# Attention stage of a three-block kernel: other slots for the head scaling, the weight chunks, the operand stacks and the big loads

## The chip, the cores and the metric

The kernel runs on one core of one Trainium2 chip. The metric is the device time of one execution in microseconds (us); lower is better. Engines are named as in the profile: PE (TensorE matmul), PEld (its weight load), DVE (VectorE), ACT (ScalarE), POOL (GpSimd), SP (SyncE, which here only issues DMAs).

## What is computed

Four sequences of 576 tokens go through attention with 8 heads of size 64, then a gated block that mixes over tokens, then a block with a low-rank token mixing and a wide feed-forward. The change touches the first block alone, and the conversion of the next block's weights that runs beside it.

```python
def _attn_ref(q, k, v):                      # (4, 8, 576, 64) each
    q_rot, k_rot = (rotate(q), rotate(k))    # rotary embedding
    scores = scale * np.matmul(q_rot, k_rot.transpose(0, 1, 3, 2))
    scores = scores - np.max(scores, axis=-1, keepdims=True)
    attn = np.exp(scores)
    attn = attn / (np.sum(attn, axis=-1, keepdims=True) + 1e-09)
    return np.matmul(attn, v)

def reference(...):
    x = attn_out.transpose(0, 2, 1, 3).reshape(B, S, H * D)
    x = _moe_ref(x=x, ...)     # h = gelu(x @ w_in); u * (w_sg @ norm(v) + b_sg); x + gated @ w_out
    return _moe2_ref(x=x, ...) # x + U V mixing over tokens, then x + relu(x @ w_ch1) @ w_ch2
```

## The kernel before

**Slots.** The attention stage has 32 heads, of 5 key chunks each (128 keys, the last 64). Its work is written out by hand in slots: head h takes slots 5h to 5h+4, and the loop over t runs from -20 to 162. In slot t PE does the scores of chunk t (`scores`, L245: the tile st), the row maxima of a tile 11 slots ahead (`row_max`, L216: the tile sm; DVE reduces it on L221) and the product with the values of the chunk three slots back (`values`, L273: pv). Row maxima of head h thus begin about slot 5h-11. Everything else is entered with `later(slot, fn)` and is issued at the end of its slot, in the order in which it was entered. A slot fixes only the order on each engine's queue; an engine runs its queue in order, and as early as its waits let it.

**PSUM.** The tiles st and sm share three buffers, so a scores matmul waits for the DVE maximum of the slot before it.

**One head's operands.** `load(h)` brings 576 KB into one of four buffers RAW. POOL rotates it in three steps (`rope`, L148 to L150). `stacks` then makes the stacked operands in three more steps: `high` rounds it on ACT (L162, tile K1) and has SP copy it twice (L163, L164); `low` subtracts on POOL (L167, tile K2), and SP copies K1 onto its own lower half (L168) and K2 into Q1 (L169); a last DMA writes a row of -1 (L173). The copy of K1 onto itself must wait until L163 and L164 have been read. Row maxima of the head need both copies of `low`. The six slots are 5h minus `LEAD`. `load(h)` is at slot 5h-30.

**A pair's scaling.** When the second head of pair i is through, at slot 10i+12 (t0), `finish` has SP gather the sums (`collect`, L304, two DMAs into rc); then POOL adds 1e-9 (`guard`, L307), DVE inverts (L310), SP writes the row to DRAM (L313) and reads it back spread over 64 partitions (L318, tile rb), and DVE scales the two heads (`apply`, L325, tile X). The slots after t0 are `INVERSE`; the second `apply` is one slot behind the first.

**Weights.** Eight chunks of w_in (512 KB each, doubles) and three smaller ones are loaded (L342) and converted: ACT (L71), DVE four times (L72 to L75), ACT (L350), POOL (L351). Chunk i loads in slot `MATRIX + APART * i` and its first step is `CONVERT` slots later. `raw64` has one buffer.

**SP is one queue.** All these DMAs but the row of maxima (L226, issued by ACT) stand in a single row on SP; if one waits for its data, all behind it wait.

After slot 162 the next block begins; from there on the order of all engines but PE is made by a scheduler.

Of the kernel before, what the change touches and what calls it, by code (L numbers as in the profile page):

```python
# [11 lines left out]
U32 = mybir.dt.uint32  # L12
# [17 lines left out]

LEAD = 23, 22, 19, 19, 15, 10
LEAD_IN = (-20, -19, -19, -8, -8, 1), (-19, -18, -16, -3, -1, 4), (-3, -3, 0, 2, 4, 8)
FIRST = (-17, -10), (-9, -9)

BY_ACT = (0, 1, 1, 1, 1), (1, 1, 0, 1, 1), (1, 0, 1, 1, 1)

LOAD, LOAD_FIRST, LOAD_V, SPLIT_V, SPLIT_V_FIRST = 30, -19, 16, (6, 1), (-11, -1)


AHEAD, RAMP_FROM, RAMP, MAX_1, ROW, ROW_0, ROW_1 = 11, -1, 25, -1, 2, -8, -9

INVERSE = 6, 8, 9, 12, 17

MATRIX, APART, CONVERT, ROWS = 12, 13, 5, (151, 159)


IDLE = 17, 2, 5, 0, 2, 5, 6, 1, 0, 1
# [3 lines left out]
def tile_kernel(ctx: ExitStack, tc: tile.TileContext, qk, vv, tabs, w_in, g_ln, wsgT, b_sg, w_out, u_r, v_r, w1, w2, out):  # L53
    nc = tc.nc

    def f(ap):
        return ap.bitcast(F32)
# [95 lines left out]
    def stacks(h, ticks):  # L153

        rot = RAW[h % NR][:, 0]
        K1, Q1, K2, Q2 = (t[h % NS] for t in (K1s, Q1s, K2s, Q2s))
        a, z = slice(0, D), slice(D, P)

        def high():
            nc.scalar.activation(K1, rot, AF.Copy)  # L162
            nc.sync.dma_start(f(Q1[a]), f(K1[z]))  # L163
            nc.sync.dma_start(f(Q2[a, 0:S]), f(K1[z]))  # L164

        def low():
            nc.gpsimd.tensor_tensor(K2, rot, f(K1), ALU.subtract)  # L167
            nc.sync.dma_start(f(K1[z]), f(K1[a]))  # L168
            nc.sync.dma_start(f(Q1[z]), f(K2[z]))  # L169
        if h < len(BY_ACT):  # L170
            steps = rope(nc.gpsimd, h) + first_stacks(h)
        else:
            steps = rope(nc.gpsimd, h) + (high, low, lambda: nc.sync.dma_start(f(K2[D:D + 1]), less_one))  # L173
            value_stacks(h)
        for tick, fn in zip(ticks, steps):
            later(tick, fn)
# [103 lines left out]
    def finish(h, t0):  # L280


        i = h // 2
        b, pr = divmod(i, NPAIR)
        o = (h % 2) * D
        pv = PVS.pop(h)[:, :, :HALF]
        if i < NP - 1:
            STAGE[h] = p1.tile([D + 1, S], F32, tag="stage", name=f"stage{h}", bufs=5)
            nc.scalar.activation(h2(STAGE[h]), pv[:D + 1], AF.Copy)
            sums = STAGE[h][D:D + 1]  # L290
        else:
            nc.scalar.activation(h2(X[b][o:o + D, pr]), pv[:D], AF.Copy)
            sums = STAGE[h] = p1.tile([1, S], F32, tag="stage", name=f"sums{h}", bufs=5)
            nc.vector.tensor_copy(h2(sums), pv[D:D + 1])  # L294
        if h % 2 == 0:
            return
        pool = p1 if i < NP - 1 else keep
        rc = pool.tile([P, 2 * S // P], F32, tag="rc", name=f"rc{i}", bufs=2 if i < NP - 1 else 1)
        rr = dram.tile([1, 2 * S], F32, tag="rr", name=f"rr{i}", bufs=2)

        def collect():
            for a in range(2):
                src = STAGE[h - 1 + a]
                nc.sync.dma_start(rc[a * D:(a + 1) * D], src[src.shape[0] - 1:])  # L304

        def guard():
            nc.gpsimd.tensor_scalar_add(rc, rc, 1e-9)  # L307

        def invert():
            nc.vector.reciprocal(rc, rc)  # L310

        def gather():
            nc.sync.dma_start(rr, rc)  # L313

        def spread():
            if i < NP - 1:
                RB[i] = p1.tile([D, 2, S], F32, tag="rb", name=f"rb{i}", bufs=1)
                nc.sync.dma_start(RB[i].rearrange("p a s -> p (a s)"), rr.to_broadcast([D, 2 * S]))  # L318
            else:
                for a in range(2):  # L320
                    nc.sync.dma_start(RB[i][a * D:(a + 1) * D], rr[:, a * S:(a + 1) * S].to_broadcast([D, S]))

        def apply(a):
            rows = slice(a * D, (a + 1) * D)
            nc.vector.tensor_tensor(X[b][rows, pr], STAGE.pop(h - 1 + a)[:D], RB[i][:, a], ALU.mult)  # L325

        def apply_last():
            nc.vector.tensor_tensor(X[b][:, pr], X[b][:, pr], RB[i], ALU.mult)
        later(t0, collect)
        for tick, fn in zip(INVERSE, (guard, invert, gather, spread)):  # L330
            later(t0 + tick, fn)
        if i < NP - 1:
            for a in range(2):
                later(t0 + INVERSE[4] + a, lambda a=a: apply(a))
        else:
            later(t0 + INVERSE[4], apply_last)

    def converted(t0, src, n, use):

        raw = p1.tile([P, 512, 2], U32, tag="raw64", name="raw64", bufs=1)[:, :n]  # L340
        t = p1.tile([P, 512], F32, tag="t64", name="t64", bufs=1)[:, :n]
        later(t0, lambda: nc.sync.dma_start(raw.rearrange("p n w -> p (n w)"), src))  # L342
        for j, fn in enumerate(from_f64(t, raw) + use(t)):
            later(t0 + CONVERT + j, fn)
# [28 lines left out]
    def later(t, fn):  # L373
        due.setdefault(t, []).append(fn)
# [31 lines left out]
    for h in range(2, NH):  # L406
        stacks(h, LEAD_IN[h - 2] if h < 5 else [NC * h - o for o in LEAD])
    for h in range(NR, NH):
        later(max(NC * h - LOAD, LOAD_FIRST + h), lambda h=h: load(h))
    WTICK = [MATRIX + APART * i for i in range(2 * KT + 3)]  # L410
    for i in range(2 * KT):
        w_in_chunk(WTICK[i], i)
# [504 lines left out]
```

## Time and profile before

| | |
|---|---|
| median of 3 runs | 968.64 us (966.61 to 969.42) |
| the profiled execution | 968.37 us, its span 966.6 us |
| PE busy | 929.6 us, 96% of the span |
| PEld / DVE / POOL / ACT busy | 81% / 54% / 40% / 36% of the span |
| attention stage | about 34 us (first scores) to 321 us (last pv) |

Busy shares are means over stages that differ. In the attention stage DVE and POOL are busy most of the time, and many short waits follow each other; so the stage is read by its period per head and by what ends PE's waits in it. A wait is put down to the engine whose signal came last; it is only as good as that guess, and SP's row of DMA issues has to be read beside it.

### The profile page before, as it was taken

The numbers are of one execution on the slowest core, as the hardware profiler recorded it, in microseconds if no ns is written. First come the engines' busy times: TensorE is split into PE (matmuls) and PEld (weight loads), VectorE is DVE, ScalarE is ACT, GpSimd is POOL, SyncE is SP. The second block draws the span as 40 slices with busy tenths as digits, with TensorE's granted clock in tenths as the row PEclk, the third lists the DMA queues.
The fourth block names the chain that finished last, engine by engine and source line by source line (L and its number), as shares of the span: only waits on it lengthen the run. The fifth ranks groups of instructions, "written<-read, shape, count | busy, mean of one in ns | idle before, by whom it ended". The sixth has DMA issues, their size and how long they took to land.

```text
span 966.6 us, 13198 instructions
## 1 busy us (share of the span) xinstructions
PE 929.6 (96%) x5180; PEld 784.4 (81%) x5180; DVE 524.3 (54%) x721; ACT 345.8 (36%) x550; POOL 382.6 (40%) x324
## 2 busy tenths in 40 slices
PE   6899998998999999999999899999999999999998
PEld 3687776777777898999999787888888888888887
DVE  7777787787875387333327945652652452222222
ACT  4366655665566453322315432321321230101000
POOL 7768776887852396232326542210210210000000
PEclk7899999999999999999999999999999999999999
DMA  5567868778751320000003001220220210000112
GB/s 174 149 180 167 203 167 187 185 176 196 170 138 38 109 79 1 1 1 1 23 23 109 22 22 44 90 85 1 82 93 1 66 44 0 1 1 22 44 49 82
DMA packets 58947, 78.00 MB, mean 81 GB/s; under 512 B 31403, under 2 KB 34758, under 8 KB 58886
## 3 DMA queue, kind: packets, MB, share of 16 engines
q1 hardware_dynamic: 58576, 77.08, 29.8%
q8 instruction: 41, 0.67, 0.3%
q14 instruction: 20, 0.16, 0.1%
q10 hardware_dynamic: 310, 0.08, 0.0%
HBM read 55.02 MB, written 4.79 MB: 62 GB/s over the span
## 4 chain that ended last, share of the span: by engine, by line
PE 73%; DVE 12%; DMA 8%; issue 3%; POOL 2%; ACT 1%; SPq 1%; ACTq 0%; DVEq 0%; POOLq 0%
PE a L544 20%; PE r L544 20%; PE pv L273 9%; PE st L245 6%; PE w L544 5%; DMA Q<-K 4%; PE m L544 3%; PE u L544 3%; PE v L544 3%; PE sm L216 3%; DVE MX L221 2%; DMA raw<-in_qk 2%; DVE X L325 1%; DVE t L74 1%; DVE g L625 1%
## 5 line engine op out<-in xcount | busy, mean ns | idle before, releaser
L221 DVE TENSOR_REDUCE MX<-sm 128x1 f32<-128x576 f32 (+1 forms) x160 | 118.6, 747 | 62.0 <-PE sm L216 59.4
L273 PE MATMUL pv<-pc,VV 128*65 128x288 f32 x512 | 144.8, 405 | 0.5 <-DVE sums L294 0.5
L245 PE MATMUL st<-Q,K 65*128 65x288 f32 (+3 forms) x640 | 126.8, 320 | 6.3 <-DVE MX L221 4.8
L245 PEld LDWEIGHTS st<-Q,K 65*128 65x128 f32 (+3 forms) x640 | 96.0, 179 | 20.0 <-DVE MX L221 7.5
L736 ACT ACTIVATE RH<-r 128x1024 fp32r<-128x1024 f32 (+1 forms) x38 | 35.5, 935 | 207.2 <-PE r L544 207.2
L737 DVE SCALAR_TENSOR_TENSOR RL<-r,RH 128x1024 fp32r<-128x1024 f32 (+1 forms) x38 | 42.3, 1112 | 123.8 <-ACT RH L736 123.7
L248 ACT ACTIVATE pc<-st 128x576 f32<-128x576 f32 x128 | 82.6, 646 | 67.7 <-PE st L245 65.8
L752 DVE TENSOR_TENSOR X<-a,X 128x256 f32<-128x256 f32 (+4 forms) x65 | 46.4, 744 | 90.8 <-PE a L544 90.7
L216 PE MATMUL sm<-K,Q 128*128 128x288 f32 (+1 forms) x320 | 77.4, 327 | 16.6 <-ACT Q L192 5.4
L544 PE MATMUL a<-RH,setB 128*128 128x512 f32 (+1 forms) x320 | 93.3, 368 | 0.0
L273 PEld LDWEIGHTS pv<-pc,VV 128*65 128x65 f32 x512 | 68.6, 137 | 29.5 <-DVE sums L294 0.7
L544 PE MATMUL a<-RH,setA 128*128 128x512 f32 (+1 forms) x288 | 83.8, 367 | 0.0
L544 PE MATMUL r<-UH,setA 128*128 128x512 f32 (+1 forms) x256 | 73.1, 364 | 0.1
L544 PE MATMUL r<-UH,setB 128*128 128x512 f32 (+1 forms) x256 | 73.2, 363 | 0.0
L216 PEld LDWEIGHTS sm<-K,Q 128*128 128x128 f32 (+1 forms) x320 | 50.9, 184 | 27.4 <-ACT Q L192 5.9
L544 PEld LDWEIGHTS a<-RH,setB 128*128 128x128 f32 x320 | 58.2, 188 | 10.0
L508 POOL TENSOR_TENSOR setB<-t,setB 128x512 fp32r<-128x512 f32 x16 | 20.7, 1296 | 102.9 <-ACT setB L697 91.7
L544 PEld LDWEIGHTS a<-RH,setA 128*128 128x128 f32 x288 | 52.1, 188 | 9.0
L544 PE MATMUL a<-RL,setB 128*128 128x512 f32 (+1 forms) x160 | 58.9, 368 | 0.0
L148 POOL TENSOR_TENSOR raw<-raw,tab 128x576 f32<-128x576 f32 x30 | 48.2, 1607 | 19.1 <-DMA raw<-in_qk 19.0
L149 POOL TENSOR_TENSOR raw<-raw,tab 128x576 f32<-128x576 f32 x31 | 51.6, 1664 | 5.1 <-DMA raw<-in_qk 5.1
L544 PEld LDWEIGHTS r<-UH,setA 128*128 128x128 f32 x256 | 46.1, 188 | 8.2 <-DVE X L678 0.4
(170 smaller groups left out, 1964.0 us busy)
## 6 DMA issues: line engine op xcount, KB each, us to landing
raw<-in_qk SPq DMA_DIRECT2D x31, 576.0 KB
Q<-K SPq DMA_DIRECT2D x87, 144.0 KB
raw<-in_w SPq DMA_DIRECT2D x24, 512.0 KB
VV<-in_vv SPq DMA_DIRECT2D x32, 160.0 KB
rb<-rr SPq DMA_DIRECT2D x15, 288.0 KB
K<-K SPq DMA_DIRECT2D x29, 144.0 KB
raw<-in_w_in SPq DMA_DIRECT2D x8, 512.0 KB
gt<-in_w SPq DMA_DIRECT2D x8, 512.0 KB
```

The source lines that it names most:

```text
L148: lambda: e.tensor_tensor(raw[:, 0], raw[:, 0], tab[:, 0], ALU.mult),
L149: lambda: e.tensor_tensor(raw[:, 1], raw[:, 1], tab[:, 1], ALU.mult),
L216: nc.tensor.matmul(ps[:TS[t], n, :HALF], Q1[:, t * P:t * P + TS[t]], K1[:, n * HALF:(n + 1) * HALF], start=True, stop=True)
L221: nc.vector.tensor_reduce(MXs[h % 2][:TS[t], t:t + 1], ps[:TS[t], :, :HALF], AX.XY, ALU.max)
L245: nc.tensor.matmul(ps[:kk, n, :HALF], l[:, c * P:c * P + kk], r[:, ns], start=st, stop=not st)
L248: nc.scalar.activation(h2(pc[:kk]), ps[:kk, :, :HALF], AF.Exp, scale=0.125)
L273: nc.tensor.matmul(o, l, r, start=(c == 0 and j == 0), stop=(c == NC - 1 and j == len(pr) - 1))
L508: return nc.gpsimd.tensor_tensor(out, a, b, ALU.subtract)
L544: nc.tensor.matmul(o, l, rr, start=(j == 0), stop=(j == n - 1))
L736: nc.scalar.activation(RH[:, s], ps[:, :, :WIDE[blk]], AF.Relu)
L737: nc.vector.scalar_tensor_tensor(RL[:, s], ps[:, :, :WIDE[blk]], 0.0, f(RH[:, s]), ALU.max, ALU.subtract)
L752: nc.vector.tensor_tensor(X[b][:, e2, xs], ps[:, :n, us], X[b][:, e2, xs], ALU.add)
```

## The change

Only slots and one buffer change; no instruction is added or taken away.

- `LEAD` 23, 22, 19, 19, 15, 10 becomes 26, 25, 23, 19, 17, 11: the rotation two to four slots earlier, `high` where it was, `low` with its copies two slots earlier, the row of -1 one slot earlier.
- In `low` the copy of K2 into Q1 is issued ahead of the copy of K1 onto itself.
- `INVERSE` 6, 8, 9, 12, 17 (and 18) becomes 3, 5, 6, 9, (14, 16).
- Weight chunks every 10 slots from slot 9 instead of every 13 from slot 12, converted 11 slots after their load instead of 5; `raw64` has two buffers.
- `load(h)` is one slot earlier from head 9 on; it stands one slot behind `low`'s copies and two ahead of `high`'s, where it was between both. (The old lower limit `LOAD_FIRST` never took effect.)

```diff
-LEAD = 23, 22, 19, 19, 15, 10
+LEAD = 26, 25, 23, 19, 17, 11
...
-INVERSE = 6, 8, 9, 12, 17
-
-MATRIX, APART, CONVERT, ROWS = 12, 13, 5, (151, 159)
+INVERSE = 3, 5, 6, 9, (14, 16)
+
+MATRIX, APART, CONVERT, ROWS = 9, 10, 11, (151, 159)
...
             nc.gpsimd.tensor_tensor(K2, rot, f(K1), ALU.subtract)
+            nc.sync.dma_start(f(Q1[z]), f(K2[z]))
             nc.sync.dma_start(f(K1[z]), f(K1[a]))
-            nc.sync.dma_start(f(Q1[z]), f(K2[z]))
...
-                later(t0 + INVERSE[4] + a, lambda a=a: apply(a))
+                later(t0 + INVERSE[4][a], lambda a=a: apply(a))
...
-        raw = p1.tile([P, 512, 2], U32, tag="raw64", name="raw64", bufs=1)[:, :n]
+        raw = p1.tile([P, 512, 2], U32, tag="raw64", name="raw64", bufs=2)[:, :n]
...
-        later(max(NC * h - LOAD, LOAD_FIRST + h), lambda h=h: load(h))
+        later(NC * h - LOAD - (h > 2 * NR), lambda h=h: load(h))
```

SP's queue through one pair of heads, before (the last number of a name counts the program's tiles):

```order
L137 DMA raw_91<-in_qk 128x2x576
L163 DMA Q_3_103<-K_3_98 64x576
L164 DMA Q_3_113<-K_3_98 64x576
L313 DMA rr_537<-rc_536 128x9
L304 DMA rc_731<-stage_631 64x1x9
L304 DMA rc_731<-stage_729 64x1x9
L142 DMA VV_118<-in_vv 128x5x64 x2
L318 DMA rb_783<-rr_537 64x1152
L173 DMA K_2_107<-less_one 1x16x36
L168 DMA K_3_98<-K_3_98 64x576
L169 DMA Q_3_103<-K_3_108 64x576
L137 DMA raw_92<-in_qk 128x2x576
```

The same queue now, a pair later:

```order
L313 DMA rr_734<-rc_733 128x9
L173 DMA K_3_108<-less_one 1x16x36
L137 DMA raw_89<-in_qk 128x2x576
L342 DMA raw_163<-in_w_in 128x1024
L163 DMA Q_0_100<-K_0_95 64x576
L164 DMA Q_0_110<-K_0_95 64x576
L318 DMA rb_925<-rr_734 64x1152
L304 DMA rc_934<-stage_834 64x1x9
L304 DMA rc_934<-stage_932 64x1x9
L168 DMA Q_0_100<-K_0_105 64x576
L169 DMA K_0_95<-K_0_95 64x576
L142 DMA VV_119<-in_vv 128x5x64 x2
```

The spreading read (rb) stood close behind the write that it waits for (rr), right ahead of `low`'s copies; now a load, a weight chunk and `high`'s copies lie between the two, and every chunk stands between a load and `high`'s copies.

DVE's queue around a pair's scaling, before:

```order
L221 TENSOR_REDUCE MX_115<-sm_0_1070 128x1
L325 TENSOR_TENSOR X_66<-stage_631,rb_982 64x576
L256 TENSOR_TENSOR ph_1068<-pt_1066,ph_1068 64x576
L221 TENSOR_REDUCE MX_115<-sm_1_1087 128x1
L224 CAST mt_1092<-sm_1_1087 5x128
L325 TENSOR_TENSOR X_66<-stage_729,rb_982 64x576
L310 RECIPROCAL rc_929<-rc_929 128x9
L221 TENSOR_REDUCE MX_115<-sm_2_1110 128x1
```

The same place now:

```order
L221 TENSOR_REDUCE MX_116<-sm_2_1220 128x1
L325 TENSOR_TENSOR X_66<-stage_834,rb_1126 64x576
L221 TENSOR_REDUCE MX_116<-sm_3_1245 128x1
L310 RECIPROCAL rc_1135<-rc_1135 128x9
L221 TENSOR_REDUCE MX_116<-sm_4_1261 64x1
L325 TENSOR_TENSOR X_66<-stage_932,rb_1126 64x576
L221 TENSOR_REDUCE MX_115<-sm_0_1279 128x1
L256 TENSOR_TENSOR ph_1277<-pt_1275,ph_1277 64x576
L221 TENSOR_REDUCE MX_115<-sm_1_1299 128x1
L224 CAST mt_1304<-sm_1_1299 5x128
```

Both scalings and the inverse stood around the subtraction ph (L256, once a head), between three maxima; now one of them stands between each two maxima, and none beside ph.

## Rows read from the trace of the kernel before

**Rows 1.** One stretch: us, busy (instructions) of PE, PEld, DVE, ACT, POOL; clock, DMA share, GB/s.

```profile
43.79:77.80 34.01, 34.01 (x206) 27.50 (x204) 23.37 (x35) 21.59 (x39) 24.61 (x22) 1.00 0.69 180
```

**Rows 2.** Chain of waits, start and us: the values of heads 0, 4 and 28.

```profile
43.79 1.50 PE pv L273 x8
...
77.80 1.49 PE pv L273 x8
...
298.25 1.49 PE pv L273 x8
```

**Rows 3.** What PE and its weight load waited for, 77.8 to 300: total, times, longest.

```profile
PE sm L216 <- ACT t L71: 2.2, 1, 2.2
PE sm L216 <- DMA Q<-K: 1.8, 4, 0.6
PE sm L216 <- ACT ph L254: 1.5, 1, 1.5
PE st L245 <- DMA Q<-mt: 1.3, 1, 1.3
...
PEld st L245 <- DVE MX L221: 7.5, 11, 1.2
```

**Rows 4.** DVE by operation, 80 to 290: count, busy us, mean ns, idle before.

```profile
L256 DVE TENSOR_TENSOR ph<-pt,ph 64x576 fp32r<-64x576 f32 x23 | 28.5, 1238 | 3.2 <-ACT ph L254 2.6
L325 DVE TENSOR_TENSOR X<-stage,rb 64x576 f32<-64x576 f32 x24 | 24.6, 1025 | 0.4
L221 DVE TENSOR_REDUCE MX<-sm 64x1 f32<-64x576 f32 x23 | 17.2, 749 | 19.3 <-PE sm L216 19.3
L224 DVE CAST mt<-sm 5x128 fp32r<-5x128 f32 x23 | 6.2, 269 | 0.0
L73 DVE TENSOR_SCALAR t<-t 128x512 uint32<-128x512 uint32 x7 | 5.5, 783 | 0.0
L310 DVE RECIPROCAL rc<-rc 128x9 f32<-128x9 f32 x11 | 2.4, 216 | 0.3
```

**Rows 5.** DVE, then PE, in order of time around one scaling: start, us.

```profile
235.89 1.86 DVE L325 TENSOR_TENSOR X<-stage,rb 64x576 f32<-64x576 f32 x1
...
238.66 0.80 PE L245 MATMUL st<-Q,K 128*128 128x288 f32 x4 [1.01 <-DVE MX L221]
```

**Rows 6.** SP's DMA issues, start and us; then PE's first maximum of that head.

```profile
126.98 0.36 SPq L313 DMA_DIRECT2D rr<-rc  x1
127.39 1.15 SPq L304 DMA_DIRECT2D rc<-stage  x2
...
132.36 0.48 SPq L318 DMA_DIRECT2D rb<-rr  x1
...
133.58 0.58 SPq L168 DMA_DIRECT2D K<-K  x1
...
137.44 0.50 PE L216 MATMUL sm<-K,Q 128*128 128x288 f32 x2 [0.56 <-DMA Q<-K]
```

**Rows 7.** SP's issues at two heads: nothing big ahead of L164, then a load and a chunk.

```profile
45.37 0.74 SPq L164 DMA_DIRECT2D Q<-K  x1
...
49.04 0.47 SPq L168 DMA_DIRECT2D K<-K  x1
...
80.21 0.65 SPq L164 DMA_DIRECT2D Q<-K  x1
...
86.45 0.47 SPq L168 DMA_DIRECT2D K<-K  x1
```

**Rows 8.** POOL in order of time: the subtraction of head 4, and a guard.

```profile
38.64 1.42 POOL L167 TENSOR_TENSOR K<-raw,K 128x576 fp32r<-128x576 f32 x1 [6.16 <-ACT K L162]
...
132.86 0.24 POOL L307 TENSOR_SCALAR rc<-rc 128x9 f32<-128x9 f32 x1 [0.21 <-DMA rc<-stage]
```

**Rows 9.** What PE waited for behind the stage, 321 to 385.

```profile
PE w L544 <- POOL GL L508: 1.3, 1, 1.3
PE m L544 <- POOL WSL L508: 1.0, 1, 1.0
```

More of the change, by code (lines that the diff above doesn't have):

```diff
@@ L37 @@
 BY_ACT = (0, 1, 1, 1, 1), (1, 1, 0, 1, 1), (1, 0, 1, 1, 1)
-LOAD, LOAD_FIRST, LOAD_V, SPLIT_V, SPLIT_V_FIRST = 30, -19, 16, (6, 1), (-11, -1)
+LOAD, LOAD_V, SPLIT_V, SPLIT_V_FIRST = 30, 16, (6, 1), (-11, -1)
 AHEAD, RAMP_FROM, RAMP, MAX_1, ROW, ROW_0, ROW_1 = 11, -1, 25, -1, 2, -8, -9
-INVERSE = 6, 8, 9, 12, 17
-MATRIX, APART, CONVERT, ROWS = 12, 13, 5, (151, 159)
+INVERSE = 3, 5, 6, 9, (14, 16)
+MATRIX, APART, CONVERT, ROWS = 9, 10, 11, (151, 159)
 IDLE = 17, 2, 5, 0, 2, 5, 6, 1, 0, 1
@@ L333, in finish @@
             for a in range(2):
-                later(t0 + INVERSE[4] + a, lambda a=a: apply(a))
+                later(t0 + INVERSE[4][a], lambda a=a: apply(a))
         else:
-            later(t0 + INVERSE[4], apply_last)
+            later(t0 + INVERSE[4][0], apply_last)
     def converted(t0, src, n, use):
-        raw = p1.tile([P, 512, 2], U32, tag="raw64", name="raw64", bufs=1)[:, :n]
+        raw = p1.tile([P, 512, 2], U32, tag="raw64", name="raw64", bufs=2)[:, :n]
         t = p1.tile([P, 512], F32, tag="t64", name="t64", bufs=1)[:, :n]
```

## The prediction

> **What bounds the kernel now.** I read the busy time by stretches first, then the chain of waits, then what ended PE's waits, and last SP's and DVE's rows in order of time beside those waits. From 43.79 to 77.80 us PE is never idle, at a granted clock of 1.00 [rows 1]; the chain gives heads 0 and 4 there [rows 2]. That is 34.01 us for four heads, 8.50 us a head, 1.70 us a slot, and it is what PE's own work costs. From head 4 to head 28 the chain takes 220.45 us [rows 2], where 24 x 8.50 is 204.1. So **16.4 us** of the stage are lost between 78 and 298 us, all after the first weight chunk and the first scaling. Nothing in the change shortens PE's work: these 16.4 us, and what PE waits for behind the stage, are all there is to win.
>
> The loss has two parts. Eleven waits of the scores end on a DVE maximum: 7.5 us at the weight load, which includes the refill of PE's pipeline [rows 3]. The rest, 8.9 us, belongs to seven waits, six of a first maximum (sm) and one of the scores: 2.2 + 1.8 + 1.5 + 1.3 = 6.8 us idle [rows 3], and about 0.3 us of refill at each. Two of these seven are put down to ACT, but SP's row shows another thing. The read rb is issued at 132.36, 5.4 us after the write rr that it waits for; the copy of K1 follows only at 133.58, and PE waits for the landing until 137.44 [rows 6]. The same order (rr, sums, values, rb, then low's copies) stands in every pair, so I put all seven down to SP: low's copies have four slots (6.8 us) from their slot to the first maximum, and POOL's subtraction (1.4 us [rows 8]), two issues and a landing of 3.9 us (133.58 to 137.44 [rows 6]) use them up. Any wait ahead on SP shows at PE.
>
> **The change part by part.**
>
> *DVE's slots.* A maximum costs 0.75 us, the row's cast 0.27, ph 1.24, a scaling 1.03, the inverse 0.22 and a conversion step about 0.78 [rows 4]. A slot gives 1.70 us. Before, DVE has between three maxima: 0.75 + 1.03 + 1.24 = 3.02, then 0.75 + 0.27 + 1.03 + 0.22 = 2.27, together 5.29 in two slots of 3.40: DVE is 1.9 us behind, more where a conversion step falls in. A wait there averages 7.5 / 11 = 0.7 us, so PE bears about 1.2 us of such lag. Now the worst place is the last conversion step beside ph: 0.75 + 0.78 + 1.24 = 2.77, a lag of 1.1 us; every scaling has a slot for itself (1.78, a lag of 0.1). The whole pair of slots with a chunk is 10 x 0.75 + 2 x 0.27 + 0.22 + 2 x 1.24 + 2 x 1.03 + 4 x 0.78 = 15.9 us of 17.0, where a chunk every 13 slots made it 15.2. So DVE fits, but with little room. At mean durations no wait is left. But a scaling has taken 1.86 us [rows 5]; where ph takes that, the lag is 1.7 and PE waits 0.5. I take this for four of the eleven chunks: 2.0 us left of 7.5. Bounds: 0 and 7.5 (as before); the case beyond that is a rival.
>
> A rule of the Trainium skill speaks against this. SBUF — State Buffer, section "SBUF: two separate sides", says that DVE operations with two SBUF inputs and GpSimd operations take one port pair by an exclusive lock, and the loser waits for the whole instruction. The trace agrees in kind: the mean scaling is 1.03 us, one of them took 1.86. By this rule the price depends on how often POOL is at work; it is one of the rivals.
>
> *SP's order and the stacks.* `low` moves from 15 to 17 slots ahead: six slots (10.2 us) to the first maximum instead of four, 3.4 us more. The waiting read rb now stands ahead of low's slot, and a load, sometimes a chunk, and high's copies lie between it and its write. What is new: the copy of K1 onto itself comes only two slots behind high's copies, and waits until they have landed; behind it on SP stand the values, the row of -1 and the next load. Without a big transfer ahead, L164 is issued at 45.37 and the copy that waits for it at 49.04: 3.7 us. Behind a load and a chunk it is 80.21 and 86.45: 6.2 us [rows 7]. From high's slot to the first maximum are eight slots, 13.6 us; ACT's rounding (21.59 / 39 = 0.55 [rows 1]) and two issues (0.6 to 0.7 each [rows 6, 7]), about 1.9 us, the wait, the issue of the copy (0.5) and its landing (3.9) make 10.0 us in the first case, 12.5 in the second. So the first head of a pair has 3.6 us to spare, and the second, with a chunk ahead, 1.1 us. I take 2.0 us left of 8.9: in eight pairs with a 512 KB chunk a wait of refill size, 0.25 us. Bounds: 0 and 8.9.
>
> *Loads.* A load has five slots (8.5 us) to its first rotation instead of seven. Were the cover gone, POOL would idle up to 3.4 us a head more; but POOL's work is 24.61 us in four heads, 12.3 a pair [rows 1], and a chunk's subtraction is one more of the 1.4 us kind [rows 8]: 13.7 of 17.0, so 3.3 us a pair may be lost before PE sees it. Nothing for it, inside the bounds above. In the ramp POOL rotates head 5 before it ends head 4; POOL then waits 6.16 us for ACT [rows 8], which hides that.
>
> *Chunks, second buffer.* Loads stand 11 slots ahead of their first use, not 5: ACT no longer waits for one at the head of its queue. Same bytes; a pair moves 2 x 576 + 8 x 144 + 2 x 160 + 288 + 512 = 3424 KB in 17.0 us, 206 GB/s; at 180 GB/s the share was 0.69 [rows 1], so about 0.79. It fits.
>
> *Behind the stage.* The last pair's read rb no longer waits behind the sums of heads 30 and 31, and the scheduler's order of DVE, ACT and POOL differs in its first rows. PE's two longest waits there are 2.3 us together [rows 9]. Both loads of the token weights now stand behind the last rr, which may cost as much. I take 0.5 us gained, between 2.5 gained and 2 lost. Later stages keep their order on PE: nothing.
>
> **Sum,** from the profiled execution (968.37 us, 0.3 below the median): 968.4 - (7.5 - 2.0) - (8.9 - 2.0) - 0.5 = **955.5 us**, 1.3% less.
>
> **The rivals.**
>
> *The second head of each pair stays tied to the big transfers.* Its copies wait 6.2 us [rows 7] in each of eight pairs instead of now and then, and the spreading read adds its 288 KB. If that eats the 1.1 us and 0.9 more, eight waits of 1.2 us with their refill make 9.4 us of copies instead of 2.0: 962.9 us. Against it: the row at 86.45 is that case already, and PE has no wait of sm as long as 1.2 us that it explains. DMA: Bandwidth & Descriptors, section "Queues, rings and completion order", says that each DMA engine takes descriptors in ring order, so what stands behind a load and a chunk starts after them. By that rule this rival is certain to cost the 6.2 us on SP; the trace agrees with the ordering, and only the slack decides.
>
> *The scaling's chain gets too short.* Sums to guard has three slots, 5.1 us; from the first issue at 127.39 to the guard at 132.86 is 5.5 us [rows 6, 8]. So POOL will wait there. If the delay runs on through rr (5.4 us to rb [rows 6]) to the scaling, DVE stands at L325 with the maxima behind it. One us in each of 14 pairs is 14 us: 969.5, no change. Against it: 14 slots, 23.8 us, for 5.5 + 5.4 us, a few issues, and a read that in rows 5 and 6 never held DVE (0.4 us idle ahead of L325 in all [rows 4]).
>
> *DVE becomes the bound, slower than before.* If the four two-input operations of a pair (ph, scaling) take 1.86 us [rows 5] instead of 1.14 on average, a pair with a chunk is 15.9 + 2.9 = 18.8 us against 17.0; eleven chunks make 20 us, and with 2 us of copies the loss is 22 instead of 16.4: 968.4 + 5.6 - 0.5 = 973.5. It decides from a mean of 1.41 us (15.9 + 4 x 0.27 = 17.0). For it: POOL gets busier per us as the heads get faster. Against it: POOL was as busy in the rows that made the mean.
>
> **How the numbers follow.** The forecast has 0.73, the tied copies 0.11 (both faster), the chain 0.09 (the same), DVE 0.07 (slower). About 0.3%, 2.9 us, can be told from no change here. So faster 0.84, same 0.09, slower 0.07. The range runs from 951, where both terms vanish and the next stage gives 1.5 us (968.4 - 16.4 + 0.5 - 1.5), to 965, which takes in the tied copies and 2 us lost behind the stage; what lies above it is 0.16, below it a little.
>
> **What would show it.** Right: heads 4 to 28 take 208 us in the chain (204.1 + 4.0), the maxima end two or three waits of the scores instead of eleven, sm waits for copies at most in second heads, and the DMA share rises to about 0.8. Wrong in the first step: waits on MX as before, ph and the scaling at over 1.4 us. Wrong in the second: rb still waits on SP ahead of low's copies, or sm waits stay at seven. The chain rival would show as idle time of DVE ahead of L325 or L310. A slower clock than 1.00 in the stage, or a later stage that moves by more than 2 us, would be outside all of this.

## The result, and the profile after

| | median | runs | ratio to before, 95% |
|---|---|---|---|
| before | 967.62 us | 965.64 to 969.42 (4) | |
| after | 976.88 us | 975.85 to 978.74 (4) | 1.0098 [1.0071, 1.0125] |

The changed kernel is 1% slower; I had forecast 955.5 us and 1.3% faster. The profiled execution of after took 976.96 us (span 975.1). The difference lies in the attention stage: from the end of head 28 to the end of the span, after takes 0.7 us less than before.

Chain of waits of after (start, us): the values of heads 4 and 28, against [rows 2].

```profile
78.08 1.49 PE pv L273 x8
...
307.45 1.49 PE pv L273 x8
```

Those 24 heads take 229.37 us instead of 220.45 and instead of the 208 that I expected. At 8.50 us a head, 25.3 us are lost where 16.4 were. Two views split the 8.9 us. First the stretch between the same two heads' ends, of before and then of after (us, busy of PE, PEld, DVE, ACT and POOL, then PE's clock, DMA share, GB/s):

```profile
79.30:299.70 220.40, 208.73 (x1225) 165.19 (x1225) 170.28 (x240) 132.56 (x234) 159.71 (x135) 1.00 0.72 173
```

```profile
79.60:309.00 229.40, 213.29 (x1226) 168.96 (x1226) 173.53 (x245) 132.25 (x237) 161.33 (x134) 0.97 0.68 163
```

PE is idle for 16.1 us (229.40 - 213.29) instead of 11.7, which is 4.4 more; and the same matmuls keep it busy 4.6 us longer, at a granted clock of 0.97 instead of 1.00. So half of the added loss is waiting, and half comes with a slower clock. What PE and its weight load waited for in after, 77.8 to 310, against [rows 3]:

```profile
PE pv L273 <- ACT stage L289: 13.5, 7, 3.7
PE st L245 <- DMA Q<-mt: 1.9, 1, 1.9
PE st L245 <- DVE mt L224: 0.6, 2, 0.3
PE sm L216 <- DMA K<-K: 0.2, 1, 0.2
```

All but one of the waits that I had counted are gone: at PE no scores wait on a maximum, and the first maxima wait 0.2 us in all; the one wait of the scores for a row of maxima (Q<-mt) is left, 1.9 us where it was 1.3. In their place stand seven waits of 0.6 to 3.7 us that before did not have, of the values for the copy out of the PSUM tile before them (L289, `stage`, on ACT). DVE has a new wait too (operations of after, 80 to 299, against [rows 4]; the numbers after the second bar are the idle time ahead):

```profile
L325 DVE TENSOR_TENSOR X<-stage,rb 64x576 f32<-64x576 f32 x24 | 23.0, 957 | 12.4 <-DMA rb<-rr 11.9
L256 DVE TENSOR_TENSOR ph<-pt,ph 64x576 fp32r<-64x576 f32 x23 | 22.4, 975 | 1.2 <-ACT ph L254 0.4
```

Where both come from is seen on SP. Waits of SP's queue for high's copies at the copy of K1 onto itself, before (L168) and after (L169), 79 to 309:

```profile
SPq L168 <- DMA Q<-K: 40.5, 16, 4.6
```

```profile
SPq L169 <- DMA Q<-K: 60.4, 24, 4.4
```

One pair of after in order of time (start, us): DVE's inverse; SP's queue; then the scaling on DVE, the guard of the next pair on POOL, and ACT.

```profile
157.13 0.20 DVE L310 RECIPROCAL rc<-rc 128x9 f32<-128x9 f32 x1
```

```profile
160.75 0.46 SPq L168 DMA_DIRECT2D Q<-K  x1
164.88 0.46 SPq L169 DMA_DIRECT2D K<-K  x1
165.45 0.77 SPq L313 DMA_DIRECT2D rr<-rc  x1
166.27 0.54 SPq L173 DMA_DIRECT2D K<-less_one  x1
166.86 0.57 SPq L137 DMA_DIRECT2D raw<-in_qk  x1
167.48 0.47 SPq L342 DMA_DIRECT2D raw<-in_w_in  x1
168.04 0.47 SPq L163 DMA_DIRECT2D Q<-K  x1
168.61 0.55 SPq L164 DMA_DIRECT2D Q<-K  x1
169.26 0.54 SPq L318 DMA_DIRECT2D rb<-rr  x1
169.85 1.48 SPq L304 DMA_DIRECT2D rc<-stage  x2
171.93 0.49 SPq L168 DMA_DIRECT2D Q<-K  x1
175.80 0.49 SPq L169 DMA_DIRECT2D K<-K  x1
```

```profile
176.75 0.75 DVE L325 TENSOR_TENSOR X<-stage,rb 64x576 f32<-64x576 f32 x1 [3.24 <-DMA rb<-rr]
```

```profile
177.28 0.32 POOL L307 TENSOR_SCALAR rc<-rc 128x9 f32<-128x9 f32 x1 [2.55 <-DMA rc<-stage]
```

```profile
172.21 0.68 ACT L162 ACTIVATE K<-raw 128x576 fp32r<-128x576 f32 x1
177.00 0.70 ACTq L226 DMA_DIRECT2D Q<-mt  x1
177.75 0.65 ACT L289 ACTIVATE stage<-pv 65x576 f32<-65x576 f32 x1 [4.87 <-DVE X L325]
```

The inverse is ready at 157.33, but its write rr is issued at 165.45, 8.1 us later. In between SP issues what stands ahead (the row of -1, a load, high's copies), is held 1.1 us at K2's copy until POOL has subtracted, and then 3.7 us at K1's copy; rr stands right behind that one. The read rb is issued at 169.26, behind the load, a chunk and high's copies, and lands only just ahead of 176.75; the sums of the next pair, issued behind it, land just ahead of 177.28. DVE waits for the one and POOL for the other. Over all pairs between 80 and 285 us, rr goes out 6.8 us behind its inverse on average, against 1.1 in before, and rb has landed 17.0 us behind it, against 10.4; the nine slots from the inverse to the first scaling are 15.3 us. In before SP was held at K1's copy too, for 40.5 us, but four or five other DMAs stood between that copy and rr.

The hold is what its row says it is: each of the 22 times in after that SP stood still at K1's copy for over 0.25 us ended within 0.1 us of the landing of the second of high's copies (L164). It also feeds itself: SP then comes late to the next head's high copies, which go out 2.8 us behind ACT's rounding on average, up to 6.2, and so land late as well.

ACT waits too: its row of maxima (L226), due behind the rounding that ended at 172.89, is issued at 177.00. The trace gives the completion semaphore of every DMA: there are eight, handed out in turn to the DMAs of SP and ACT, and from 40 us on none of 357 goes out before the one that had the same semaphore has landed. For L226 that is here a copy of the sums. In all seven waits of PE, L226 was issued within 0.1 us of the last signal of such a copy, and within 0.3 us of a guard, after standing still for up to 4.1 us. The row names a scaling of DVE (L325) as what L289 waited for. L289 does not depend on it; ACT's queue was held by the DMA ahead of it. The profile does not print that hold. That fits what the Trainium skill says in Perfetto Trace Analysis, section "DMA Instruction — HWDGE (DVE, Sync)": the reported start of a DMA is the moment at which all its semaphores are satisfied, so the wait lies ahead of the row. Here the 4.1 us between 172.89 and 177.00 are indeed nobody's.

Then the clock. Three stretches of after around this wait, same columns as above:

```profile
170.00:174.50 4.50, 4.50 (x30) 3.69 (x27) 3.45 (x5) 2.21 (x4) 3.83 (x4) 1.00 1.02 288
174.50:178.40 3.90, 0.21 (x2) 0.00 (x0) 1.54 (x3) 0.65 (x2) 1.27 (x3) 1.00 0.60 128
178.50:183.00 4.50, 4.50 (x17) 3.26 (x17) 2.76 (x3) 2.44 (x5) 3.97 (x4) 0.62 0.89 209
```

And one group of four matmuls ahead of it and behind it:

```profile
171.73 1.13 PE L273 MATMUL pv<-pc,VV 128*65 128x288 f32 x4
...
181.38 1.89 PE L273 MATMUL pv<-pc,VV 128*65 128x288 f32 x4
```

PE was busy all of 4.50 us, then stood nearly still for 3.90, and in the next 4.50 us got through 17 matmuls instead of 30 at a mean clock of 0.62: part of the stretch ran at 1.2 instead of 2.4 GHz. So a wait of 3.7 us cost PE some 5.4: 4.50 x 0.38 = 1.7 us come on top. Before had no such stretch between 79 and 300 us; after has four. The first of them came behind the wait of 1.9 us for a row of maxima:

```profile
104.00:107.40 3.40, 3.40 (x14) 2.48 (x14) 0.94 (x2) 1.20 (x2) 3.32 (x3) 0.56 0.24 47
```

### The profile page after: what moved, and what is told of

It reads as the page before. It is cut to its first block, busy times and chain, and to the rows that moved or that the text cites. A ratio compares the mean times of both kernels' runs of the same rounds, so it can differ in the third digit from the quotient of the medians.

```text
span 975.1 us, 13193 instructions
## 1 busy us (share of the span) xinstructions
PE 933.6 (96%) x5179; PEld 788.8 (81%) x5180; DVE 525.0 (54%) x721; ACT 345.2 (35%) x550; POOL 385.8 (40%) x324
## 4 chain that ended last, share of the span: by engine, by line
PE 75%; DVE 9%; DMA 8%; issue 3%; POOL 2%; ACT 2%; SPq 1%; ACTq 0%; POOLq 0%; DVEq 0%
PE a L544 20%; PE r L544 20%; PE pv L273 11%; PE st L245 6%; DMA rb<-rr 5%; PE w L544 5%; PE sm L216 3%; PE m L544 3%; PE u L544 3%; PE v L544 3%; DVE g L625 1%; DVE MX L221 1%; DVE t L74 1%; DMA Q<-mt 1%; PE t L648 1%
## 5 line engine op out<-in xcount | busy, mean ns | idle before, releaser
L273 PE MATMUL pv<-pc,VV 128*65 128x288 f32 x512 | 148.6, 414 | 13.9 <-ACT stage L289 13.5
L273 PEld LDWEIGHTS pv<-pc,VV 128*65 128x65 f32 x512 | 69.2, 139 | 45.8 <-ACT stage L289 15.3
L148 POOL TENSOR_TENSOR raw<-raw,tab 128x576 f32<-128x576 f32 x30 | 45.9, 1530 | 37.2 <-DMA raw<-in_qk 37.2
L544 PE MATMUL a<-RL,setA 128*128 128x512 f32 (+1 forms) x144 | 52.7, 366 | 0.0
```

Source lines behind the costliest of these rows:

```text
L148: lambda: e.tensor_tensor(raw[:, 0], raw[:, 0], tab[:, 0], ALU.mult),
L273: nc.tensor.matmul(o, l, r, start=(c == 0 and j == 0), stop=(c == NC - 1 and j == len(pr) - 1))
L544: nc.tensor.matmul(o, l, rr, start=(j == 0), stop=(j == n - 1))
```

## The experiments

Fifteen kernels, in the order in which they ran. "SP's hold" is always the wait in the fences above: SP at the copy of K1 onto itself until high's copies have landed, 79 to 309 us. "Loss" is the time between the ends of heads 4 and 28 less the 204.1 us of 24 heads without waits. Both are read from the profiled execution of each kernel, while the times given are medians; before itself had medians of 965.7 to 967.6 us beside them, so two kernels are best compared by their ratios to before.

### Relieving those who wait

I first took the traces at their word and relieved the engines that wait. A in the first texts is the reading that ACT, held at its row of maxima, costs the time; B, that DVE, held at the scaling, does.

**The scaling two slots and one slot later** (in after):

```diff
-INVERSE = 3, 5, 6, 9, (14, 16)
+INVERSE = 3, 5, 6, 9, (16, 17)
```

> The two scalings of a pair stand 16 and 17 slots behind it instead of 14 and 16, all else as in the changed kernel. Theory A (ACT's DMA of the row of maxima waits for the sums' landing, and the copy of the values behind it frees PE's tile): DVE's wait for rb (11.9 us in six waits) goes to under 2 us, but PE's waits for the stage copy stay at 11 to 14 us, and the time at 974 to 978. Theory B (the stage copy, and so PE, waits for the scaling, as the profile guesses): the scaling now stands behind rb's landing, PE's waits for the stage copy fall below 4 us, and the time to 958 to 964.

975.62 us, 1.0092 [1.0055, 1.0129]. DVE no longer waits for rb, but PE still waits 12.1 us (5 times) for the stage copy, and DVE now 7.2 us (4) for the guard at L310. B falls.

**No row of maxima on ACT** (left out from head 9 on; lines behind it are one higher):

```diff
-            later(tick + 1, lambda: nc.scalar.dma_start(row, f(mt)))
+            if done < 9:
+                later(tick + 1, lambda: nc.scalar.dma_start(row, f(mt)))
```

> From head 9 on the row of maxima is not sent to the operands (ACT issues no such DMA; the old row stands there), all else as in the changed kernel. Theory A: nothing holds ACT ahead of the stage copy, PE's waits for it go to zero; DVE's waits for rb stay (8 to 12 us) but PE bears about 1.2 us of each, so 3 to 5 us of PE waits for maxima come in their place; without the long waits PE's clock stays at 1.00. Time 957 to 964. Theory B: PE's waits for the stage copy stay over 10 us, time 972 to 977.

977.01 us, 1.0105 [1.0073, 1.0138]: a miss for A as well. The waits for the stage copy are gone, which bears out that the row of maxima is what held ACT, but the time did not move. PE's first wait and DVE's, of this kernel:

```profile
PE st L246 <- DVE MX L221: 13.5, 9, 2.8
```

```profile
DVE X L326 <- DMA rb<-rr: 25.4, 9, 4.1
```

What ACT's hold had hidden now stands in DVE: it waits for rb with the maxima behind it, and PE waits for those, 13.5 us: as much as it had waited for the stage copy.

**The scaling's old slots** (in after: rr and rb later, both scalings beside ph again):

```diff
-INVERSE = 3, 5, 6, 9, (14, 16)
+INVERSE = 6, 8, 9, 12, (17, 18)
```

> The slots of the scaling's chain are the old ones (6, 8, 9, 12, 17, 18), all else as in the changed kernel. The spreading read now stands behind the sums and low's copies on SP. If the shorter chain is what costs (both theories): PE's waits for the stage copy fall below 3 us, the waits of the scores for maxima come back in part (3 to 8 us), time 957 to 966. If the chunks or the stacks cost: 972 or more.

982.80 us, 1.0169 [1.0131, 1.0207], a miss: slower still, so the longer chain does not win back what is lost. Waits on maxima are back (7.0 us, 11), with 6.0 us for ph; SP's hold stays at 55.7 us.

**The old chunks** (in after):

```diff
-MATRIX, APART, CONVERT, ROWS = 9, 10, 11, (151, 159)
+MATRIX, APART, CONVERT, ROWS = 12, 13, 5, (151, 159)
...
-        raw = p1.tile([P, 512, 2], U32, tag="raw64", name="raw64", bufs=2)[:, :n]
+        raw = p1.tile([P, 512, 2], U32, tag="raw64", name="raw64", bufs=1)[:, :n]
```

> The weight chunks are the old ones (every 13 slots from slot 12, converted 5 slots behind their load, one buffer), all else as in the changed kernel. If the chunk between the load and high's copies is what makes the sums and rb land late: their landing comes about 2.5 us earlier in the pairs that had a chunk, DVE's wait for rb falls from 11.9 to under 4 us, PE's waits for the stage copy from 13.5 to under 5 us, time 960 to 966. If the K1 copy that holds SP ahead of the write rr, and the load, are enough by themselves: waits stay at 9 to 13 us, time 970 to 976.

973.13 us, 1.0073 [1.0049, 1.0097]. The stage waits are a little fewer (10.4 us, 7), SP's hold 53.9 us. So the chunks' new places are not the cause; whether they add to it is not shown, since the interval overlaps that of after.

**Both relieved at once** (the row of maxima left out from head 9 on, and a later scaling):

```diff
-INVERSE = 3, 5, 6, 9, (14, 16)
+INVERSE = 3, 6, 6, 9, (16, 17)
...
+            if done < 9:
+                later(tick + 1, lambda: nc.scalar.dma_start(row, f(mt)))
```

> Both waits taken away at once: from head 9 on no row of maxima is sent (as in the run without it), the scalings stand 16 and 17 slots behind their pair, and the inverse one slot later (6 instead of 5), so that DVE waits neither for rb nor for the guard. Theory C (the sums and rb land together, 0.2 us apart, and each alone holds PE; hence neither run with one of them away gained): DVE's waits for rb and for the guard fall under 4 us, no wait for a stage copy, at most 6 us of waits in heads 5 to 28, time 955 to 962. If something else holds PE too (the K1 copies, the loads): 968 or more.

977.58 us, 1.0109 [1.0059, 1.0159]: another miss of its first branch. No wait for the stage copy or rb is left; now the first maxima wait for the copies (5.3 us, 8). SP's hold is 55.9 us.

**Sums, rr and rb issued by ACT instead of SP** (in after).

```diff
-                nc.sync.dma_start(rc[a * D:(a + 1) * D], src[src.shape[0] - 1:])
+                nc.scalar.dma_start(rc[a * D:(a + 1) * D], src[src.shape[0] - 1:])
...
-            nc.sync.dma_start(rr, rc)
+            nc.scalar.dma_start(rr, rc)
...
-                nc.sync.dma_start(RB[i].rearrange("p a s -> p (a s)"), rr.to_broadcast([D, 2 * S]))
+                nc.scalar.dma_start(RB[i].rearrange("p a s -> p (a s)"), rr.to_broadcast([D, 2 * S]))
```

> Slots as in the changed kernel, nothing left out; only the three small transfers of the scaling's chain (sums, rr, rb) are issued by ACT, whose queue has no loads, chunks or operand copies in it. Theory C with its cause (they land 7 us after their issue because a load, a chunk and four copies stand ahead of them on SP's queue, and rr is issued 8 us after its inverse because the K1 copy holds SP): sums and rb land 3 to 4 us after their issue, the waits for rb and for the stage copy go, time 952 to 960. If the DMA engines are simply full, and any queue is as late: waits as in the changed kernel, 970 to 978. If ACT's queue is now held by rr and rb instead: waits of ACT for DMAs, PE waits for exponentials, 966 to 980.

975.69 us, 1.0101 [1.0074, 1.0128]. The scaling's transfers are free of SP, but ACT's own queue is held by them: PE waits 7.0 us (3) for ACT's exponentials and 5.2 us (11) on maxima. The third branch holds. SP's hold is 52.9 us. The Trainium skill, DMA: Bandwidth & Descriptors, section "Issuing engines are not separate DMA queues", says that DMAs started from several engines run on the same 16 DMA engines, and that only issue time is saved. The time did not fall, but the trace shows more saved than issue time (2.8 us for these four DMAs in the rows above): rb had landed 10.3 us behind its inverse on average instead of 17.0, since it no longer stood behind SP's hold. What that gained was lost at ACT.

Six kernels within 10 us of each other, each with other waits at PE and with 53 to 65 us of the same hold on SP: whoever is relieved, the next in line waits. That pointed at the hold itself.

### The stacks

**All of the stacks put back** (in after):

```diff
-LEAD = 26, 25, 23, 19, 17, 11
+LEAD = 23, 22, 19, 19, 15, 10
...
-            nc.sync.dma_start(f(Q1[z]), f(K2[z]))
             nc.sync.dma_start(f(K1[z]), f(K1[a]))
+            nc.sync.dma_start(f(Q1[z]), f(K2[z]))
```

> The slots of the stacks are the old ones (low 15 slots ahead, K1 copied ahead of K2), all else as in the changed kernel. The K1 copy is then four slots behind high's copies, not two, and holds SP less. Theory C: rr leaves SP 3 to 4 us earlier, so rb and the sums land 2 to 4 us earlier; waits for rb and the stage copy fall to a third, while waits of first maxima for copies come back (up to 6 us); time 962 to 970. If the K1 copy's place does not matter: 974 to 978 and more.

955.93 us, 0.9899 [0.9867, 0.9931]: 21 us less than after, and 1% faster than before. SP's hold falls to 1.8 us (5), rb holds DVE nowhere, and the loss is 6.4 us.

**Only the stacks changed** (in before).

```diff
-LEAD = 23, 22, 19, 19, 15, 10
+LEAD = 26, 25, 23, 19, 17, 11
...
+            nc.sync.dma_start(f(Q1[z]), f(K2[z]))
             nc.sync.dma_start(f(K1[z]), f(K1[a]))
-            nc.sync.dma_start(f(Q1[z]), f(K2[z]))
```

> The kernel before with the new slots of the stacks and the new order of low's two copies, nothing else. By the prediction's copies term alone (8.9 to 2.0 us) the time is 958 to 962. If the K1 copy two slots behind high's copies holds SP, and with it rr and rb, also with the old slots of the chain: DVE or ACT wait for them, 965 to 975.

975.42 us, 1.0101 [1.0063, 1.0139]: just above the range of the second branch; they alone cost what the whole change costs. With the old slots of the chain rr does not stand right behind K1's copy (it goes out 1.8 us behind its inverse on average), so the hold costs by other ways: POOL waits 45.1 us (19) for loads, DVE 10.3 us (8) for rb, and PE 11.4 us (8) for maxima. SP's hold of this kernel:

```profile
SPq L169 <- DMA Q<-K: 69.8, 22, 6.0
```

### Which part of the stacks

Four kernels made from after, and a fifth in between, tell apart theory S (SP's hold at K1's copy two slots behind high's copies), R (the earlier rotation) and O (the swapped order).

**Only low back at 15 slots ahead.**

```diff
-LEAD = 26, 25, 23, 19, 17, 11
+LEAD = 26, 25, 23, 19, 15, 10
```

> The changed kernel, with only low (subtraction, K2 copy, K1 copy) put back to 15 slots ahead and the row of -1 to 10; the rotation stays two to four slots earlier, and K2's copy stays ahead of K1's. Theory S (what costs is the copy of K1 onto itself two slots behind high's copies: it holds SP until they have landed, and rr, the load, rb and the sums stand behind it): 954 to 962, as with all of the stacks put back (955.9), and SP waits at that copy for a landing less than 10 us in all between 79 and 309 us instead of 60. Theory R (what costs is the earlier rotation: POOL waits for loads and its guard comes late): no better than the change, 972 to 979.

956.74 us, 0.9915 [0.9881, 0.9948]. No hold is left. S holds, and R falls as the main cause.

**Only the order of low's copies back** (K1 onto itself first).

```diff
-            nc.sync.dma_start(f(Q1[z]), f(K2[z]))
             nc.sync.dma_start(f(K1[z]), f(K1[a]))
+            nc.sync.dma_start(f(Q1[z]), f(K2[z]))
```

> The changed kernel, with only the order of low's two copies put back (K1 onto itself first, then K2 into Q1), all slots as changed. Theory S: 974 to 979, since the copy that waits still stands two slots behind high's copies; SP then waits for the landing about as long, now ahead of K2's copy as well. Theory O (the swapped order is what costs, since K1's copy now has the later place): 954 to 962.

997.68 us, 1.0319 [1.0250, 1.0389]. O falls, and S missed the size by 19 us. SP's hold and PE's first wait of this kernel:

```profile
SPq L168 <- DMA Q<-K: 99.5, 28, 6.0
```

```profile
PE pv L273 <- ACT stage L289: 29.3, 10, 4.2
```

With K1's copy first, the hold begins a DMA earlier and K2's copy stands behind it too. PE is idle for 31.1 of 254.8 us (80.5 to 335.3, clock 0.93), and eight stretches between these heads are partly at the lower clock. At 17 slots the new order is thus a gain.

**Only the copy of K1 onto itself two slots later.**

```diff
             nc.sync.dma_start(f(Q1[z]), f(K2[z]))
+            if h < 5:
+                own()
+        def own():
             nc.sync.dma_start(f(K1[z]), f(K1[a]))
...
+            if h > 4:
+                later(ticks[4] + 2, own)
```

> The changed kernel, with the subtraction and K2's copy left 17 slots ahead, and the copy of K1 onto itself alone put two slots later (15 ahead), from head 5 on. Theory S in its narrow form (that one DMA's wait on SP is the whole loss): 954 to 962, SP's wait at it for a landing under 15 us instead of 60. Theory R (the rotation) or one by the place of the subtraction: 972 to 979. Between, 963 to 971, if K2's copy, which itself stands where SP may wait for POOL, carries a part.

964.10 us, 0.9971 [0.9953, 0.9989]: the branch between. About 13 of the 21 us go with that one DMA. The hold is 1.4 us (2). K2's copy, which stayed at 17, holds SP for POOL much as in after (22.1 us, 11, put down to a step of the values there; the rows show it issued 0.03 us behind the end of the subtraction). The first maxima wait 7.0 us in nine waits, and each of them ends 0.1 to 0.3 us behind the landing of K1's copy: at 15 slots that copy stands behind the load and the chunk. One was issued at 122.20 and landed at 129.73, and the maximum began at 129.98.

**Only the rotation back at 23, 22 and 19.**

```diff
-LEAD = 26, 25, 23, 19, 17, 11
+LEAD = 23, 22, 19, 19, 17, 11
```

> The changed kernel, with only the three steps of the rotation put back to 23, 22 and 19 slots ahead; low and its copies stay 17 ahead. Theory S: 972 to 979, with SP's wait at the copy of K1 still at 45 to 65 us. Theory R: 954 to 962, with POOL's wait for the loads gone.

971.94 us, 1.0045 [1.0020, 1.0069]. The time is at S's lower end; the hold is smaller than expected:

```profile
SPq L169 <- DMA Q<-K: 28.8, 21, 4.5
SPq L168 <- POOL K L167: 23.5, 11, 2.7
```

SP stands at K2's copy 26.5 us in all, little longer than in after (21.0). But with the later rotation it waits 21.1 us (20) at L163 for ACT's rounding, where after waits 2.6 (4): high's copies go out at once behind the rounding, and land 4.6 us after their issue on average instead of 5.8, which leaves less to wait for at K1's copy. Some 5 us of the 21 thus go with the earlier rotation; by which way was not tested.

**Low at 16 slots ahead.**

```diff
-LEAD = 26, 25, 23, 19, 17, 11
+LEAD = 26, 25, 23, 19, 16, 10
```

> The changed kernel, with low at 16 slots ahead (the change has 17, the kernel before 15) and the row of -1 at 10: the copy of K1 onto itself then stands three slots behind high's copies instead of two or four. Theory S (SP is held at that copy until they land): between the two, 957 to 966, with 5 to 30 us of SP's wait for a landing there between 79 and 309 us, and few of PE's waits put down to the stage copy. If the loss were not that wait but the place of the subtraction on POOL, 970 to 978 with less than 5 us of SP's wait.

953.74 us, 0.9859 [0.9832, 0.9886]: a miss on the good side, and the best of all. Heads 4 to 28 take 205.6 us. SP's hold, what the weight load waited for, the stretch, and the write rr with the read rb of the same pair as above:

```profile
SPq L169 <- DMA Q<-K: 2.5, 4, 1.0
```

```profile
PEld st L245 <- DVE MX L221: 1.4, 5, 0.3
```

```profile
79.30:284.90 205.60, 205.40 (x1227) 164.51 (x1226) 178.99 (x245) 132.57 (x236) 165.51 (x134) 1.00 0.70 180
```

```profile
149.82 0.19 DVE L310 RECIPROCAL rc<-rc 128x9 f32<-128x9 f32 x1
```

```profile
150.04 0.35 SPq L313 DMA_DIRECT2D rr<-rc  x1
152.17 0.46 SPq L168 DMA_DIRECT2D Q<-K  x1
152.73 0.54 SPq L169 DMA_DIRECT2D K<-K  x1
...
157.49 0.55 SPq L318 DMA_DIRECT2D rb<-rr  x1
```

PE is busy for 205.40 of 205.60 us, at a clock of 1.00. The inverse ends at 150.01 and rr goes out at 150.04. Over all pairs rb has landed 11.8 us behind the inverse, inside the 15.3 of its slots. One slot does two things here: the hold goes, and rr, which at 17 slots stands right behind K1's copy, now stands ahead of low's copies. No run moved rr alone, so what each of the two gives was not told apart; but with the old slots of the chain (982.8 and 975.4 us) rr did not stand right behind that copy either, and the loss was there. SP still waits, 24.3 us (20) at L163 for ACT's rounding and 26.5 us (14) at rr for the inverse, but there it is early for its data.

At 15 slots low's copies stand behind the load and the chunk, and PE still waited 2.4 us (4) for them (K2 first); at 17 SP is held; at 16, where they stand right ahead of the load, neither. In one line, all with the new scaling, chunks and loads:

| low's copies | SP's hold, us | loss, us | median, us |
|---|---|---|---|
| 16, K2 first | 2.5 | 1.5 | 953.7 |
| 15, K1 first, late rotation | 1.8 | 6.4 | 955.9 |
| 15, K2 first | none | 4.8 | 956.7 |
| K2 at 17, K1 at 15 | 1.4 | 11.8 | 964.1 |
| 17, K2 first, late rotation | 28.8 | 20.6 | 971.9 |
| 17, K2 first (after) | 60.4 | 25.3 | 976.9 |
| 17, K1 first | 99.5 | 50.7 | 997.7 |

### The two gains apart

**The scaling alone** (in before).

```diff
-INVERSE = 6, 8, 9, 12, 17
+INVERSE = 3, 5, 6, 9, (14, 16)
...
-                later(t0 + INVERSE[4] + a, lambda a=a: apply(a))
+                later(t0 + INVERSE[4][a], lambda a=a: apply(a))
```

> The kernel before, with the scaling's slots alone changed (3, 5, 6, 9, (14, 16)); chunks, stacks and loads as before. The forecast charged seven waits of first maxima (8.9 us) to the read rb standing ahead of low's copies; this alone takes rb away from there. If that is right, the waits of sm for copies fall from about seven to two or fewer and the time is 957 to 962. If the waits on the maxima (7.5 us) went with the scaling too, 951 to 957. If the first maxima wait as before, 964 to 969.

973.20 us, 1.0069 [1.0050, 1.0088]: slower than all three ranges. The first maxima no longer wait for the copies, as the prediction said, but the maxima still do hold PE (9.0 us, 13, at the weight load), and the stage waits come up (5.2 us, 3). One of them in this kernel, on POOL, ACT and PE:

```profile
137.94 0.24 POOL L307 TENSOR_SCALAR rc<-rc 128x9 f32<-128x9 f32 x1 [6.34 <-DMA rc<-stage]
```

```profile
139.69 0.68 ACT L162 ACTIVATE K<-raw 128x576 fp32r<-128x576 f32 x1 [4.66 <-POOL raw L150]
```

```profile
141.51 2.18 PE L273 MATMUL pv<-pc,VV 128*65 128x288 f32 x4 [4.08 <-ACT stage L289]
```

The guard stands earlier in POOL's queue and waits for sums that were issued behind a load, a chunk and rb; the rotation behind it is late, ACT's rounding waits for that, and PE for ACT.

**The chunks alone** (in before).

```diff
-MATRIX, APART, CONVERT, ROWS = 12, 13, 5, (151, 159)
+MATRIX, APART, CONVERT, ROWS = 9, 10, 11, (151, 159)
...
-        raw = p1.tile([P, 512, 2], U32, tag="raw64", name="raw64", bufs=1)[:, :n]
+        raw = p1.tile([P, 512, 2], U32, tag="raw64", name="raw64", bufs=2)[:, :n]
```

> The kernel before, with the chunks alone changed (every 10 slots from slot 9, converted 11 slots after the load, two buffers); scaling, stacks and loads as before. Chunks closer together put one conversion beside every pair: 965 to 972, the waits on the maxima no fewer than eleven, since both scalings still stand beside ph. If the single buffer had been behind the waits of the first maxima, 958 to 963.

966.84 us, 1.0002 [0.9981, 1.0023]: no change, as the first branch had it. The first maxima stop waiting here as well, which I had not expected; the waits on DVE's maxima stay (10.7 us, 11, at the weight load). Neither part is worth anything alone; both together, with the old stacks, are worth 10 us. That kernel also has the load's new slot, which no run put back or tried by itself, and no run told the chunks' slots from their second buffer.

## Why the prediction was wrong, point by point

- **DVE's slots: right in the waits, wrong in the sizes.** I left 2.0 us of waits on maxima at the weight load; after has 0.2, and the kernel with low at 16 has 1.4. But a conversion step takes about 1.18 us there, not 0.78, and ph 0.90 instead of 1.24. A pair with a chunk then sums to 7.5 + 0.5 + 0.2 + 2 x 0.90 + 2 x 1.13 + 4 x 1.18 = 17.0 us. Yet DVE is busy for only 15.9 of 17.1 us a pair there (five pairs with a chunk, 96.4 to 181.7), since in the rows most operations begin some 0.08 us ahead of the end of the one before, and the durations of these pairs sum to 16.6. So my 15.9 came out, with other terms: that is luck. The DMA share of those pairs is 0.80, as I had said; in after it is 0.71 (98 to 203). And I gave the gain to the scaling's slots; it takes the chunks' new place as well (with the scaling alone 9.0 us are left). Operations of the kernel with low at 16, 80 to 285:

```profile
L325 DVE TENSOR_TENSOR X<-stage,rb 64x576 f32<-64x576 f32 x25 | 28.2, 1126 | 0.4
L256 DVE TENSOR_TENSOR ph<-pt,ph 64x576 fp32r<-64x576 f32 x24 | 21.7, 904 | 1.5 <-ACT ph L254 0.8
...
L73 DVE TENSOR_SCALAR t<-t 128x512 uint32<-128x512 uint32 x7 | 8.3, 1191 | 0.0
L72 DVE TENSOR_SCALAR t<-t 128x512 f32<-128x512 f32 x7 | 8.3, 1186 | 0.0
```

- **SP's order and the stacks: the step that failed.** For the readers of the copies it was right: of the seven waits 0.2 us of first maxima and the 1.9 us for a row of maxima are left, where I had left 2.0. I saw that K1's copy would wait two slots behind high's copies, for 3.7 to 6.2 us [rows 7], and listed the values, the row of -1 and the next load behind it on SP. I left out rr, which in every pair stands right behind one of these copies. And I charged the wait only against the slack of its own reader, 3.6 and 1.1 us to the first maximum, and took it that SP comes to high's copies in time (ACT's rounding, which I took at the 0.55 us of ACT's mean operation, is 0.68 in the rows; that changes little). Its price is paid by those behind it in the queue, who need nothing from it: rr, then rb and the sums, then the load. SP is held 60.4 us, rr goes out 6.8 us behind its inverse, and the 21 us between after and the same kernel with the old stacks go with the place of low's copies: 956.7 us with low alone put back, 964.1 with K1's copy alone.
- **The chain rival had the right sign, not the right cause.** I gave it 0.09 and 969.5 us. As it said, DVE idles ahead of L325 (12.4 us instead of 0.4). But it laid that to the chain's shorter slots; with the old ones the changed kernel takes 982.8 us, and with the same short ones and the old stacks 955.9. My ground against it was 23.8 us for 5.5 + 5.4 us and "a few issues"; one of these few was a DMA that waits. From the inverse at 157.13 to the scaling at 176.75 it took 19.6 us. Nor had I priced that the sums' late landing holds ACT as well as POOL. Where the scaling alone is changed, the guard's shorter distance to the sums does cost, as the rival said: 973.2 us.
- **The clock was outside of the prediction**, as it said itself; the busy time that came with it is 4.6 of the 8.9 us.
- **Loads: I took nothing.** POOL waits for loads 33.6 us (21) in after and 18.4 (10) in before; with low at 16 it is 1.2 us (2). So POOL does not miss the load's longer lead where SP is not held; what its waits cost PE where SP is held was not told apart.
- **Behind the stage: about right.** From the end of head 28 on after is 0.7 us faster. PE's two longest waits from 330 to 395 us are 1.8 us together, 0.5 less than in [rows 9], which is the 0.5 that I took:

```profile
PE w L544 <- POOL GL L508: 1.3, 1, 1.3
PE w L544 <- ACT GH L626: 0.5, 1, 0.5
```

- **What stays open.** How much of the loss at each pair is rb, how much the sums and how much the load was not told apart; when one is relieved the others take its place. Nor was rr's place right behind K1's copy told from the length of the hold. That ACT is held through a shared completion semaphore is read from the semaphores and times in the trace, and the run without the row of maxima bears it out, but no run gave that DMA a semaphore of its own.

## What to carry to other kernels

A DMA that must wait for its data is charged to everything behind it on its issuing queue, not to its reader alone: for each one that is moved, find the new distance to what it waits for, and list who stands behind it and how much slack they have. The sum of a queue's waits is not their price: before held SP for 40.5 us at the same copy, and the best kernel's SP waits 50.8 us for ACT and DVE. When PE's wait moves from engine to engine as you relieve them, look for one queue that holds them all. One slot can be the whole difference: here 15 was a little late for the reader, 17 too early for the queue, and at 16 both waits went.

## What was not expected of the hardware

- A wait of PE can cost more than its length: behind one of 3.7 us a part of the next 4.5 us ran at 1.2 GHz (mean clock 0.62), and four matmuls took 1.89 us instead of 1.13. The length of the wait alone did not tell: in after such stretches came behind waits of 1.6, 1.9, 2.1 and 3.7 us, and none behind one of 2.3 us (157.48) or in before, with waits of up to 2.2.
- Transfers land late behind large ones: rb (288 KB), issued at 169.26 behind 576 + 512 + 288 KB, was there at 176.75, 7.5 us later, where it took 4.3 us on average in before; the sums (2.2 KB each), issued by 171.33 behind it, at 177.28, some 6 us later.
- DVE's operations changed their mean durations between kernels with the same work: ph from 1.24 us in before to 0.90 with low at 16, a conversion step from 0.78 to 1.19. Why was not tested.
